# Where one queue issues attention stores and expert-weight loads, in an attention + MoE + dense-max kernel

## The chip, the cores and the metric

One core of one Trainium2 chip. The metric is device time in microseconds (us) of the whole kernel: 698.57 us, median of 3 runs (698.44 to 699.79).

## The reference, cut to what matters

Three stages, chained. Attention: 4 batches, 8 heads, 576 rows, head size 64, a causal window of 128 with a linear bias per head. Its output is a [2304, 512] matrix. A mixture of experts routes each row to one of 8 experts; then a dense layer takes the maximum of three products.

```python
# attention, for each batch and head
scores = where(0 <= rel < 128, q @ k.T / 8 - slope[h] * abs(rel), -1e9)
x = softmax(scores) @ v                       # -> [2304, 512]
# experts
e_idx = argmax(x @ w_gate + bias[modality]); gate = softmax(...)[e_idx]
out[e_idx == e] = gate * (relu(x[e_idx == e] @ w1[e]) @ w2[e])     # 512 -> 1024 -> 512
# dense layer
h = max(max(x @ g1, x @ g2), x @ g3); y = h @ w_out                # 512 -> 768 -> 512
```

Products run in float16 as high and low parts, in three passes (`PASSES`), so every float32 weight is first turned into two float16 tiles.

## The kernel before, in words

The order of work on every engine is written out by hand; each engine and each queue runs its own list in that order, and semaphores hold an instruction until its inputs and its buffer are ready. Nearly all loads and stores are issued by SyncE (SP), one after another: an issue that waits for a buffer holds all that are behind it.

**Attention.** `Attention.run` makes 41 steps. A step takes one group of four heads of one 128-row tile and does a part of several groups at once. `norm` (L426), early in a step, writes the finished rows into the tile `x` on VectorE (L436) and then issues the store of `x` to the scratch matrix `xs` (L443, L448) on SP; 16 full stores and 4 pairs of small ones in all. At the end of a step the list `todo` runs: loads of raw k, q and v (L274, `load`, seven to five steps ahead of use, three buffers for each), their transposes (`turn`, L283 on TensorE), and the splitting of v.

**Experts.** Rows are sorted by expert and cut into four batches (u = 0 to 3) of one or two units each: 496 | 480, 224 | 496 | 496, 192 columns. A unit needs 8 pieces of weights of 512 KB (four of `w1`, four of `w2`), so 48 pieces, here called P0 to P47. A piece is loaded into one of three buffers `st` (L945), converted to its high part on ScalarE (L954) and to its low part on VectorE (L963, which frees the buffer). `Weights.get(n)` (L969) runs ahead of the products that use piece n (twice for a `w1` piece, once for a `w2` piece): it converts the low part of piece n+1 and the high part of piece n+2, and then issues the load up to piece n+4. A product (L991 first layer, L1010 second) is split by ScalarE (`hf` L981, then L982) and GpSimd (L983). The second layer leaves `yT` in four blocks (dm = 0 to 3), which the dense layer reads.

**Interleaving.** The units of batches 0 and 1 run between attention steps: `layer1` (L1411) makes a step about every three and a half us of expert work. Attention ends within the 480 unit; its memory is then given to the dense layer, whose 24 weight loads (here W0 to W23; L1065, L1071, `Weights2`) go through four buffers `st2` and are put together from their bits on VectorE (L1105, L1110, L1116), scaled and split on ScalarE (L1133, L1134) and GpSimd (L1135). `tick` and `finish`, called in `layer1` after each block of products, do this bit by bit; a load W is issued behind the L1116 that frees its buffer. The dense layer for batches 0 and 1 follows (products L1150, maxima L1159, output L1195), then the expert layers of batches 2 and 3, where four more buffers serve the pieces (`more`), then the second dense layer.

In SP's list, around the end of attention, the loads stand so: P18, W0 to W3, P19, W4, W5, P20 to P24, W6, W7, P25, P26, P27, W8 and so on. P25 is issued in `get(21)`, which serves dm = 1 of the 224 unit; the high parts of P24 and P25 are converted in `get(22)` and `get(23)`, on ScalarE ahead of the splits of dm = 2 and dm = 3.

Of the kernel before, what the change touches and what calls it, by code (L numbers as in the profile page):

```python
# [15 lines left out]
B, H, S, D = 4, 8, 576, 64  # L16
# [31 lines left out]
def windowed_attention_moe_kernel(  # L48
# [16 lines left out]
    nc = tc.nc  # L65
# [11 lines left out]
    xs = [dram.tile([HALF, DM], F32, name=f"xs{h}") for h in range(2)]  # L77
# [33 lines left out]
    class Bias:  # L111


        def __init__(self, pool, pf, bias, nq, widths):
            self.bias, self.nq = bias, nq
            tot = sum(widths)
            self.rf = pf
            if nq < 128:
                self.rf = pool.tile([128, 1], F32, name=f"c_rf{nq}")
                nc.vector.tensor_copy(self.rf[0:nq], pf[0:nq])  # L120
                nc.vector.tensor_scalar(self.rf[nq:], pf[nq:], float(-nq), None, ALU.add)
            self.ci = pool.tile([128, tot], I32, name=f"c_ci{nq}")
            o = 0
            for w, base in zip(widths, (-WIN, 0)):
                nc.gpsimd.iota(
                    self.ci[:, o:o + w], base=base,
                    pattern=[[1, w]], channel_multiplier=0,
                )
                o += w
            self.rel = pool.tile([128, tot], F32, name=f"c_rel{nq}")  # L130
            self.t = pool.tile([128, tot], F32, name=f"c_t{nq}")
# [88 lines left out]
    def drain(gen):  # L220
        for _ in gen:
            pass
# [29 lines left out]
    class Attention:  # L252
# [5 lines left out]
        def __init__(self, pool):  # L258
            self.p = pool
            self.bias = pool.tile([128, H, 256], BF16, name="bias", bufs=1)  # L260
            self.biast = pool.tile([128, 4, 192], BF16, name="biast", bufs=1)
            self.raw, self.qT, self.kT, self.v = {}, {}, {}, {}
            self.xs, self.got = {}, set()
            self.mixed = False
            self.outs = []

        def rows(self, t):
            return 128 if t < 4 else 64
# [157 lines left out]
        def norm(self, b, t, g, ps):  # L426
            p = self.p
            if g == 0:
                self.xs[b, t] = p.tile([128, 2, 4, D], F32, name="x", tag="x", bufs=2)
            x = self.xs[b, t]  # L430
            rd = p.tile([128, 4, 1], F32, name="rd", tag="rd", bufs=2)
            nc.vector.tensor_scalar(rd, ps[:, :, D:D + 1], SV / SX * 1e-9, None, ALU.add)
            yield
            nc.vector.reciprocal(out=rd, in_=rd)
            yield
            nc.vector.tensor_tensor(  # L436
                out=x[:, g], in0=ps[:, :, 0:D], in1=rd.to_broadcast([128, 4, D]),
                op=ALU.mult,
            )
            dst, r = xs[b // 2], S * (b % 2)  # L440
            if t == 4:
                for u in range(2):
                    nc.sync.dma_start(  # L443
                        out=dst[r + 512:r + S, 256 * u:256 * u + 256],
                        in_=x[64 * u:64 * u + 64, 0].rearrange("p b c -> p (b c)"),
                    )
            elif g == 1:
                nc.sync.dma_start(  # L448
                    out=dst[r + 128 * t:r + 128 * t + 128, :],
                    in_=x.rearrange("p a b c -> p (a b c)"),  # L450
                )

        def xt(self, t, x):
            kd = KD if t < 4 else KD // 2
# [30 lines left out]
        def run(self):  # L485
            grp = [(b, t, g) for b in range(B) for t in range(5) for g in range(2 if t < 4 else 1)]
            todo = {}

            def at(n, f, *a):
                todo.setdefault(max(n, 0), []).append((f, a))  # L490

            for n, (b, t, g) in enumerate(grp):
                if g:
                    continue
                if n >= 4:
                    for x, nm in enumerate("kqv"):
                        at(n - LEAD + x, self.load, nm, b, t)
                if n:
                    at(n - 4, self.turn, "k", b, t)
                    at(n - 3, self.turn, "q", b, t)  # L500
                at(n - 2, self.high_v, b, t)
                at(n - 2 + (n > 1), self.low_v, b, t)
            ss, es, ehl, xts, lgs, pvs = {}, {}, {}, {}, {}, []
            N = len(grp)
            for n in range(N + 5):
                norm = iter(())
                if n < N:
                    if n not in ss:
                        ss[n] = self.qk(*grp[n])
                    pvs.append(n)  # L510
                if n in lgs and (self.mixed or n >= N):
                    self.logits(*lgs.pop(n))
                    self.logits_out()
                due = [m for m in pvs if m <= n - 3]
                for m in due:
                    pvs.remove(m)
                    drain(norm)
                    self.low(ehl[m])
                    norm = self.norm(*grp[m], self.pv(*grp[m], ehl.pop(m)))
                if self.mixed and 0 <= n - 1 < N:  # L520
                    ehl[n - 1] = self.transpose(*grp[n - 1], es.pop(n - 1))
                if n < N:
                    es[n] = self.softmax(*grp[n], ss.pop(n), norm)
                if not self.mixed and n + 1 < N:
                    ss[n + 1] = self.qk(*grp[n + 1])
                for _ in norm:
                    fill()
                if n in lgs:
                    self.logits(*lgs.pop(n))
                if n - 2 in ehl:  # L530
                    self.low(ehl[n - 2])
                self.logits_out()
                if not self.mixed and 0 <= n - 1 < N:
                    ehl[n - 1] = self.transpose(*grp[n - 1], es.pop(n - 1))
                if 0 <= n - 1 < N:
                    self.high(ehl[n - 1])
                for m in due:
                    b, t, g = grp[m]
                    if g or t == 4:
                        xts.setdefault(n + (t < 4), []).append((b, t, self.xs.pop((b, t))))  # L540
                for b, t, x in xts.pop(n, ()):
                    if n + 1 in lgs:
                        self.logits(*lgs.pop(n + 1))
                    lgs[n + 1] = (b, t, self.xt(t, x))
                if self.mixed and n - 1 in ehl:
                    self.low(ehl[n - 1])
                for f, a in todo.pop(n, ()):
                    f(*a)
                yield n

        def start(self):
# [363 lines left out]
    class Weights:  # L915
# [51 lines left out]
                self.whole += 1  # L967

        def get(self, n):  # L969
            self.low(n + 2)  # L970
            self.high(n + 3)
            self.issue(n + (9 if self.more else 5))
            return self.wt[n]

    def slot(pool, wst, w0, xT, yT, d, cap):
# [163 lines left out]
    def moe2(pool, items, w, hmt, n2=C2, both=False, **kw):  # L1139
# [5 lines left out]
        def product(run, yT, c, m, i):  # L1145
            ps = psM.tile([128, 512], F32, name="m", tag="m")[:, 0:n2]
            n = 0
            for kk in range(KD):
                for wl, xl in PASSES:
                    nc.tensor.matmul(  # L1150
                        out=ps, lhsT=w.g[:, wl, i, m, kk, :],
                        rhs=yT[:, xl, kk, c:c + n2], start=(n == 0), stop=(n == 3 * KD - 1),
                    )
                    n += 1
            nx = pool.tile([128, C2], F32, name="hx", tag="hx", bufs=4)[:, 0:n2]
            if i == 0:
                nc.scalar.activation(out=nx, in_=ps, func=ACTF.Copy, scale=2.0 ** -6)
            else:
                nc.vector.scalar_tensor_tensor(  # L1159
                    out=nx, in0=ps, scalar=2.0 ** -6, in1=run, op0=ALU.mult, op1=ALU.max  # L1160
                )
            return nx
# [344 lines left out]
```

## Time and profile before

| | |
|---|---|
| median of 3 runs | 698.57 us (698.44 to 699.79) |
| the profiled execution | 693.81 us, its span 691.9 us |
| TensorE (PE) busy | 645.2 us, 93% of the span |
| VectorE (DVE) / ScalarE (ACT) / GpSimd (POOL) busy | 353.6 / 345.3 / 226.6 us |
| granted TensorE clock | 0.983 of full speed over the span |
| bytes moved | 69.95 MB, mean 101 GB/s |

Times in the rows are microseconds from the first instruction of the span. SPq is the queue of SyncE, on which the DMAs are issued. A timeline row has start, duration, engine, line, operation, output and input; in square brackets stands the idle time of the engine just before it and what ended it. The chain is the work that ended last, followed back from the last instruction.

### The profile page before, as it was taken

The page shows a single profiled execution, that of the slowest core. Times are in us where ns is not written, and L with a number is a line of the kernel's source. Part 1 is how long each engine was busy: PE and PEld are TensorE (multiplying, and loading weights), DVE is VectorE, ACT ScalarE, POOL GpSimd, SP SyncE. Part 2 cuts the span into 40 slices and gives each one's busy share as a digit, 9 for nine tenths or more (in the row PEclk, how much of TensorE's full clock was granted, in tenths as well). Part 3 has the DMA queues.
Part 4 walks back from the last instruction along what each step waited for, and adds up shares of the span by engine and source line. Part 5 has one row for each costly group of instructions (what it writes and reads, how often), then busy time and mean ns, then how long its engine had stood idle before and what let it go on. Part 6 is the DMA issues. An engine that isn't in the chain of part 4 may idle for free.

```text
span 691.9 us, 12893 instructions
## 1 busy us (share of the span) xinstructions
PE 645.2 (93%) x4787; PEld 400.0 (58%) x4787; DVE 353.6 (51%) x1083; ACT 345.3 (50%) x660; POOL 226.6 (33%) x232
## 2 busy tenths in 40 slices
PE   6899888989997999899889999999999999999993
PEld 5687755656664656755555564444447656656641
DVE  5977864666475738999981233152324455201100
ACT  5898877777584837654552211354647211111110
POOL 2111226323131315766672311482424111121121
PEclk9999999999998999999999999999999999999997
DMA  9655773545330238664733403344240000000011
GB/s 192 108 124 133 195 200 87 119 113 164 106 91 20 78 117 272 214 203 162 190 113 76 92 22 122 119 127 120 91 117 8 1 0 1 1 31 16 0 47 49
DMA packets 120800, 69.95 MB, mean 101 GB/s; under 512 B 68872, under 2 KB 115484, under 8 KB 120732
## 3 DMA queue, kind: packets, MB, share of 16 engines
q1 hardware_dynamic: 116992, 59.06, 32.3%
q0 software_dynamic: 3040, 9.96, 4.6%
q8 instruction: 40, 0.66, 0.4%
q14 instruction: 28, 0.23, 0.1%
q10 hardware_dynamic: 700, 0.04, 0.1%
HBM read 57.19 MB, written 9.44 MB: 96 GB/s over the span
## 4 chain that ended last, share of the span: by engine, by line
PE 73%; DVE 12%; ACT 6%; DMA 3%; issue 3%; POOL 0%; ACTq 0%; SPq 0%; POOLq 0%; DVEq 0%
PE m L1150 25%; PE m L991 13%; PE m L1010 12%; PE m L1195 10%; PE s L335 4%; DMA st<-in_moe_w_dram 2%; PE m L376 2%; PE m L468 2%; DVE b L1110 2%; PE m L283 2%; PE bank L406 2%; DVE e L348 2%; ACT e L357 2%; ACT eh L382 1%; DVE wt L963 1%
## 5 line engine op out<-in xcount | busy, mean ns | idle before, releaser
L1150 PEld LDWEIGHTS <-g 128*128 128x128 f16 x1296 | 127.2, 98 | 93.8 <-issue 11.3
L1150 PE MATMUL m<-yT,g 128*128 128x384 f16 x648 | 109.1, 329 | 7.3 <-DVE hx L1159 2.9
L1150 PE MATMUL m<-yh,g 128*128 128x384 f16 x648 | 105.7, 326 | 0.0
L963 DVE SCALAR_TENSOR_TENSOR wt<-st,wt 128x1024 f16<-128x1024 f32 x48 | 61.9, 1293 | 79.3 <-ACT wt L954 79.3
L1010 PE MATMUL m<-ht,wt 128*128 128x496 f16 (+3 forms) x576 | 100.3, 333 | 1.7 <-DVE el L387 1.2
L1159 DVE SCALAR_TENSOR_TENSOR hx<-m,hx 128x384 f32<-128x384 f32 x72 | 39.7, 555 | 116.7 <-PE m L1150 116.7
L991 PEld LDWEIGHTS <-wt 128*128 128x128 f16 x576 | 55.6, 99 | 55.4 <-issue 9.3
L1010 PEld LDWEIGHTS <-wt 128*128 128x128 f16 x576 | 54.6, 98 | 43.4 <-issue 2.8
L983 POOL TENSOR_TENSOR ht<-hf,ht 128x496 f16<-128x496 f32 (+3 forms) x48 | 49.5, 1036 | 89.3 <-ACT ht L982 85.7
L981 ACT ACTIVATE hf<-m 128x496 f32<-128x496 f32 (+3 forms) x72 | 35.8, 497 | 76.2 <-PE m L1010 47.5
L357 ACT ACTIVATE e<-e,nm 128x256 f32<-128x256 f32 (+2 forms) x144 | 59.2, 471 | 21.1 <-DVE nm L348 20.9
L991 PE MATMUL m<-xT,wt 128*128 128x496 f16 (+2 forms) x288 | 58.5, 347 | 7.3 <-DVE el L387 3.8
L348 DVE CUSTOM_DVE_ANT_0 e<-s,bias 128x256 f32<-128x256 f32 (+1 forms) x128 | 45.8, 382 | 19.9 <-PE s L335 11.7
L991 PE MATMUL m<-xh,wt 128*128 128x496 f16 (+1 forms) x288 | 51.1, 330 | 0.0
L954 ACT ACTIVATE wt<-st 128x1024 f16<-128x1024 f32 x48 | 50.0, 1045 | 2.0 <-DMA st<-in_moe_w_dram 1.7
L387 DVE TENSOR_TENSOR el<-m,eh 128x512 f16<-128x512 f32 x64 | 42.4, 683 | 7.1 <-ACT eh L382 7.1
L1181 POOL TENSOR_TENSOR xh<-hx,xh 128x384 f16<-128x384 f32 x18 | 16.4, 913 | 89.8 <-ACT xh L1180 89.8
L335 PE MATMUL s<-kT,qT 64*128 64x256 f32 (+2 forms) x320 | 42.2, 384 | 3.3 <-DVE nm L348 2.2
L1180 ACT ACTIVATE xh<-hx 128x384 f16<-128x384 f32 x18 | 9.4, 523 | 70.8 <-DVE hx L1159 66.9
L311 POOL TENSOR_TENSOR vl<-rawv,vh 128x512 f16<-128x512 f32 (+1 forms) x20 | 23.0, 1149 | 65.7 <-ACT vh L304 65.7
L1201 ACT ACTIVATE ob<-m,gate 128x512 f32<-128x512 f32 x18 | 12.4, 687 | 55.0 <-PE m L1195 49.6
L382 ACT ACTIVATE eh<-m 128x512 f16<-128x512 f32 x64 | 34.6, 584 | 4.3 <-PE m L376 4.1
(184 smaller groups left out, 976.3 us busy)
## 6 DMA issues: line engine op xcount, KB each, us to landing
st<-in_moe_w_dram SPq DMA_DIRECT2D x66, 512.0 KB, 4.0
rawk<-in_k_dram SPq DMA_DIRECT2D x16, 256.0 KB, 4.5
rawq<-in_q_dram SPq DMA_DIRECT2D x16, 256.0 KB, 5.1
rawv<-in_v_dram SPq DMA_DIRECT2D x16, 256.0 KB, 3.5
xs<-x SPq DMA_DIRECT2D x16, 256.0 KB, 2.2
st<-in_moe_w_out_dram SPq DMA_DIRECT2D x6, 512.0 KB, 3.9
rawk<-in_k_dram SPq DMA_DIRECT2D x4, 128.0 KB, 4.5
rawq<-in_q_dram SPq DMA_DIRECT2D x4, 128.0 KB, 3.8
```

Source lines behind the costliest of these rows:

```text
L335: nc.tensor.matmul(out=out[u][rows, x // 2, c0:c1], lhsT=self.qT[b, t][r, i, 0:n], rhs=self.kT[b][r, i, k0 + c0:k0 + c1], start=True, stop ...
L348: nc.vector.tensor_tensor_reduce(out=e[:, x, c0:c1], in0=s[x % 2][:, x // 2, c0:c1], in1=bias[:, x, c0:c1], scale=-0.125, scalar=3.0e38, o ...
L357: nc.scalar.activation(out=e[:, x, c0:c1], in_=e[:, x, c0:c1], func=ACTF.Exp, scale=-1.0, bias=nm[:, x:x + 1],)
L382: nc.scalar.activation(out=b, in_=a, func=ACTF.Copy)
L387: nc.vector.tensor_tensor(out=o, in0=a, in1=b, op=ALU.subtract)
L954: nc.scalar.activation(out=wt[:, 0], in_=st, func=ACTF.Copy, scale=SW)
L963: nc.vector.scalar_tensor_tensor(out=wt[:, 1], in0=st.rearrange("p (a b) -> p a b", a=a), scalar=SW, in1=wt[:, 0], op0=ALU.mult, op1=ALU.s ...
L983: nc.gpsimd.tensor_tensor(out=lo, in0=hf, in1=hi[1], op=ALU.subtract)
L991: nc.tensor.matmul(out=ps, lhsT=wt[:, wl, kk, o:o + 128], rhs=xT[:, xl, kk, bass.ds(d[0], cap)], start=(n == 0), stop=(n == 3 * KD - 1),)
L1010: nc.tensor.matmul(out=ps, lhsT=wt[:, wl, f, :], rhs=hs[f][:, xl], start=(n == 0), stop=(n == 3 * KF - 1),)
L1150: nc.tensor.matmul(out=ps, lhsT=w.g[:, wl, i, m, kk, :], rhs=yT[:, xl, kk, c:c + n2], start=(n == 0), stop=(n == 3 * KD - 1),)
L1195: nc.tensor.matmul(out=ps, lhsT=hm[:, xl, f, 128 * u:128 * u + 128], rhs=w.wo[:, wl, f, :], start=(n == 0), stop=(n == 3 * K2 - 1),)
```

## The change

The store of a finished attention tile is no longer issued within `norm`: `norm` puts it on a list, and a new function `store` issues all stores on the list at the end of the step, behind the loads of later tiles. `Weights.get` issues loads first instead of last, and one piece fewer: up to piece n+3 ahead of the conversions of `get(n)`, where it was up to piece n+4 behind them (with the four additional buffers up to n+7, where it was n+8).

```diff
-            self.outs = []
+            self.outs, self.stores = [], []
...
-            dst, r = xs[b // 2], S * (b % 2)
-            if t == 4:
-                for u in range(2):
+            self.stores.append((b, t, g, x))
+
+        def store(self):
+
+            while self.stores:
+                b, t, g, x = self.stores.pop(0)
+                dst, r = xs[b // 2], S * (b % 2)
+                if t == 4:
+                    for u in range(2):
+                        nc.sync.dma_start(
+                            out=dst[r + 512:r + S, 256 * u:256 * u + 256],
+                            in_=x[64 * u:64 * u + 64, 0].rearrange("p b c -> p (b c)"),
+                        )
+                elif g == 1:
                     nc.sync.dma_start(
...
                 for f, a in todo.pop(n, ()):
                     f(*a)
+                self.store()
                 yield n
...
         def get(self, n):
+            self.issue(n + (8 if self.more else 4))
             self.low(n + 2)
             self.high(n + 3)
-            self.issue(n + (9 if self.more else 5))
             return self.wt[n]
```

## Rows read from the trace of the kernel before

**Rows 1.** Busy time by stretch: length; PE, PEld, DVE, ACT, POOL; clock, DMA share, GB/s
```profile
258.00:296.00 38.00, 33.95 (x280) 24.38 (x279) 33.80 (x77) 24.34 (x45) 22.95 (x18) 1.00 0.71 225
296.00:360.00 64.00, 59.14 (x358) 34.52 (x356) 60.45 (x81) 32.76 (x61) 42.58 (x33) 0.98 0.60 179
360.00:678.00 318.00, 317.96 (x1834) 176.21 (x1833) 92.49 (x241) 100.24 (x173) 90.65 (x90) 1.00 0.19 55
```

**Rows 2.** Waits of PE, DVE, ACT, ended by loads or unexplained: total us, times, longest
```profile
PE m L283 <- DMA rawk<-in_k_dram: 4.2, 1, 4.2
...
DVE b L1105 <- DMA st<-in_moe_w_dram: 3.9, 1, 3.9
...
PE m L283 <- issue: 3.4, 2, 1.9
...
ACT wt L954 <- DMA st<-in_moe_w_dram: 1.7, 1, 1.7
```

**Rows 3.** Waits of the SP queue itself, the same columns
```profile
SPq L945 <- DVE wt L963: 175.4, 36, 21.3
...
SPq L448 <- DVE x L436: 99.6, 16, 17.4
```

**Rows 4.** Timeline around the longest store wait: SP queue, then ACT
```profile
204.56 0.37 SPq L945 DMA_DIRECT2D st<-in_moe_w_dram  x1
...
222.44 0.34 SPq L448 DMA_DIRECT2D xs<-x  x1
...
230.67 1.05 ACT L954 ACTIVATE wt<-st 128x1024 f16<-128x1024 f32 x1
```

**Rows 5.** Timeline around a transpose of raw k: SP, DVE, PE
```profile
126.71 0.66 SPq L274 DMA_DIRECT2D rawk<-in_k_dram  x1
...
150.48 0.69 DVE L387 TENSOR_TENSOR el<-m,eh 128x512 f16<-128x512 f32 x1 [0.51 <-ACT eh L382]
...
151.27 0.63 PE L283 MATMUL m<-ident,rawk 128*128 128x128 f32 x4 [1.90 <-issue]
```

**Rows 6.** The chain of waits from 284 to 302: start, us, what
```profile
285.53 6.22 DMA st<-in_moe_w_dram
...
294.98 6.07 PE m L1150 x26
```

**Rows 7.** Timeline of the SP queue behind the end of attention
```profile
258.08 2.04 SPq L1065 DMA_DIRECT2D st<-in_moe_w_dram  x4
...
264.89 0.38 SPq L945 DMA_DIRECT2D st<-in_moe_w_dram  x1
266.81 0.97 SPq L1065 DMA_DIRECT2D st<-in_moe_w_dram  x2
...
282.02 0.38 SPq L945 DMA_DIRECT2D st<-in_moe_w_dram  x1
283.80 0.98 SPq L1065 DMA_DIRECT2D st<-in_moe_w_dram  x2
...
285.53 0.38 SPq L945 DMA_DIRECT2D st<-in_moe_w_dram  x1
```

**Rows 8.** Timeline of ACT: conversions of P19, P24 and P25
```profile
271.62 1.04 ACT L954 ACTIVATE wt<-st 128x1024 f16<-128x1024 f32 x1
...
288.32 1.04 ACT L954 ACTIVATE wt<-st 128x1024 f16<-128x1024 f32 x1
...
291.77 1.06 ACT L954 ACTIVATE wt<-st 128x1024 f16<-128x1024 f32 x1 [1.74 <-DMA st<-in_moe_w_dram]
```

**Rows 9.** DMA traffic in two stretches, columns as in Rows 1
```profile
259.40:265.40 6.00, 6.00 (x32) 2.77 (x31) 3.11 (x5) 2.12 (x3) 1.04 (x1) 1.00 1.00 340
283.10:292.20 9.10, 8.16 (x77) 7.04 (x75) 9.03 (x22) 6.74 (x13) 7.62 (x5) 1.00 0.89 289
```

**Rows 10.** Timeline of DVE: low parts of P19 and P20; first dense maximum
```profile
276.06 2.77 DVE L963 SCALAR_TENSOR_TENSOR wt<-st,wt 128x1024 f16<-128x1024 f32 x2
...
301.15 0.56 DVE L1159 SCALAR_TENSOR_TENSOR hx<-m,hx 128x384 f32<-128x384 f32 x1 [0.49 <-PE m L1150]
```

More of the change, by code (lines that the diff above doesn't have):

```diff
@@ L439, in norm @@
             )
-            dst, r = xs[b // 2], S * (b % 2)
-            if t == 4:
-                for u in range(2):
+            self.stores.append((b, t, g, x))
[10 more added lines that the diff above has]
+                elif g == 1:
                     nc.sync.dma_start(
-                        out=dst[r + 512:r + S, 256 * u:256 * u + 256],
-                        in_=x[64 * u:64 * u + 64, 0].rearrange("p b c -> p (b c)"),
-                    )
[L447 to L451, printed above, removed]
+                        out=dst[r + 128 * t:r + 128 * t + 128, :],
+                        in_=x.rearrange("p a b c -> p (a b c)"),
+                    )
         def xt(self, t, x):
```

## The prediction, made before the changed kernel had run

> **What bounds the kernel now.** I read the table of busy time by stretch first, then the waits, then the chain, then the timelines of SP, ACT and DVE. From 360 us on TensorE is busy for 317.96 of 318 us [rows 1]: nothing there is won by issuing a load elsewhere, and any time lost or gained before 360 us arrives at the end in full. From 296 to 360 VectorE is busy for 60.45 of 64 us and TensorE for 59.14; in that stretch VectorE puts the dense weights together and TensorE waits for them. From 258 to 296 VectorE is again the fullest (33.80 of 38) after TensorE.
>
> The change touches only SP's list, so the question is who waits for SP. SP itself waits a lot, 175.4 us for buffers of expert weights and 99.6 us for finished attention rows [rows 3]; that looks like a prize. But the compute engines wait for a load from SP in three places only [rows 2]: 4.2 us for the first raw k at the start of the run (ahead of any store), 3.9 us for the first dense weights, and 1.7 us on ScalarE for one expert piece. The last one is on the chain: the DMA of P25, issued at 285.53, lands 6.22 us later, and the chain goes from it over ScalarE and GpSimd to the dense product that goes on at 294.98 [rows 6].
>
> **The change part by part.** It adds no instruction and takes none away; it reorders 24 stores, some 50 loads of k, q, v, and the loads from P4 on.
>
> *Stores behind the loads of their step.* Loads of raw tiles leave about a step earlier, the stores where VectorE has written the row, as before. Nothing waited for a raw tile after the start [rows 2], so the gain is nothing. Stores are read back by GpSimd's gathers much later, and [rows 2] holds no wait that a store ended: cost nothing. Ends: the third rival prices a gain; a loss would need a raw tile to be late, and none leaves later than it did.
>
> *Pieces one `get` later, while attention runs.* The buffer of a piece is free just as early as before, but in SP's list the piece now stands behind the stores of the step in between. ScalarE converts piece j in `get(j-2)`; it used to be issued in `get(j-4)` and is now in `get(j-3)`. The worst place is the store that left at 222.44: P13 left at 204.56, and will leave just behind that store, at about 222.9. With a landing as slow as the 6.22 us of [rows 6] it is there at 229.1; ScalarE converts it at 230.67 [rows 4]. The cover is 1.6 us. I take nothing; if the cover were gone (a landing half as long again, at 232.2), ScalarE and the products behind it would be late by 1.6 us.
>
> *Pieces behind the dense weights, 258 to 296.* Here SP's list holds the loads W. The new order is W0 to W3, P18, W4, W5, P19 to P23, W6, W7, P24, P25, P26: each piece that stood ahead of a batch of W now stands behind it. In the first half that costs ScalarE some waiting (second rival) that VectorE, busy with other work, hides in my reading. In the second half it meets the chain. P24 left at 282.02, W6 and W7 at 283.80, P25 at 285.53 [rows 7]. W6 waits for VectorE's L1116, so P24 will leave behind it at about 284.8; P25 still leaves at about 285.5, when its buffer is free.
>
> What P25 then costs, step by step. Between 283.1 and 292.2 the DMA engines moved 9.1 us x 289 GB/s = 2.63 MB [rows 9], which is five transfers of 512 KB (P24, W6, W7, P25, P26): 1.82 us each. P25, the fourth, had its data by 283.1 + 4 x 1.82 = 290.4 and landed at 291.75, 1.35 us later. In the new order the first of the four is W6. W0 was issued at 258.08 and data began to flow at 259.4 [rows 7, 9], so W6's data begin at 283.8 + 1.3 = 285.1; the DMA engines lie idle for the two us before. Four transfers at 1.82 us and 1.35 us to land: 293.7. At the best rate that rows show, 6.0 us for the four of W0 to W3 (340 GB/s, 1.5 us each), it is 292.45 with the same 1.35 us, and 291.1 with nothing for landing. I take 293.1, halfway between the two that count landing. P24 lands a transfer earlier, at 291.3 to 291.6, well after the 288.32 at which ScalarE converted it. From there ScalarE needs 291.77 - 1.74 - 288.32 = 1.71 us for that conversion and the split of dm = 2 [rows 8], so it is free for P25 at about 293.1 too. P25's conversion starts at 293.1 instead of 291.77: 1.3 us later. The ends are 0 (P25 there by 291.1 and P24 in time) and 2.0 us (293.7).
>
> Behind this conversion on ScalarE stands the split of dm = 3; for its two halves wait GpSimd's L983 and the dense products at 294.98. These get the 1.3 us. Does it pass on? The first maximum of the dense layer finds VectorE idle for 0.49 us, waiting for TensorE [rows 10], so VectorE has no slack to swallow it, and from there to 360 it is the full engine, in a fixed order. It passes.
>
> A rule of the Trainium skill speaks against this. The page "DMA: Bandwidth & Descriptors", section "Anatomy of one DMA", gives a transfer 2.0 us plus its bytes over 436 GB/s; in sum four transfers of 512 KB would take 4.8 us of data, P25 would land by about 291.2 and the delay would be near nothing. The rows show 1.5 to 1.82 us for each where the rule has 1.2, so I go by the rows; the first rival is the case in which the rate is better than these.
>
> *P27 and the later pieces.* P27 no longer leaves in this stretch but before the second expert layer, where SP has nothing else to do and TensorE is full [rows 1]: nothing.
>
> Sum: +1.3 us on the profiled execution, 693.81 to 695.1. The median of the runs is 698.57, 4.8 us above the profiled one; I add the same 1.3 us to it: 699.9 us.
>
> **The rivals.**
>
> First, *no change*: P24 and P25 land in time, because with P19 and P27 out of the way the DMA engines move faster than 1.5 us a transfer, or VectorE's stretch from 301 us on gives the time back. For it: the 0 end above, and 59.14 of 64 us on TensorE leave it 4.9 us of idle time that VectorE sets. Against it: the 0.49 us. Time 698.6.
>
> Second, *slower by more*: P19. It left at 264.89, ahead of W4 and W5 (266.81); it will leave behind them, at 267.9. With 1.3 us until data flow from 266.81, three transfers at 1.5 to 1.82 us and 1.35 us to land it is there between 274.0 and 274.9; ScalarE converted it at 271.62 and will wait 2.4 to 3.3 us. VectorE takes its low part at 276.06 [rows 10] and needs ScalarE's 1.04 us first, so the point from which it costs is a landing at 275.0. My estimate is just under it. If it is past by 1.5 us (a transfer more in front), VectorE, full since 262, carries that to the end beside the 2.0 us of P25: 3.5 us, 702.1.
>
> Third, *faster*: twice, 3.4 us together [rows 2], TensorE stands still ahead of a transpose of raw k with no releaser shown; the longer is the 1.90 us before 151.27 [rows 5]. If these are late loads, held behind a store, loads ahead of stores win both: 695.2. It decides at a load landing later than the start of the gap (149.4). Against it: the last raw k issued by then with time to be this one left at 126.71, 22 us before, and the gap ends 0.1 us after VectorE's L387 (150.48 + 0.69 = 151.17), which frees a PSUM buffer. That the change doesn't reach what SP waits for is part of the first rival.
>
> **How the numbers follow.** Chances: forecast 0.40 (its own range 698.8 to 700.6), no change 0.27, slower by more 0.15, faster 0.18. 0.2% of the time, 1.4 us, is about what a measurement of this kernel can tell from none. The forecast's 1.3 us lies at that bound, so it gives 0.20 to same and 0.20 to slower. No change gives 0.22, 0.03 faster and 0.02 slower. Sums: faster 0.21, same 0.42, slower 0.37. The range goes from 696.2 (short of the third rival's full gain) to 702.2 (the second rival's sum).
>
> **What would show it.** Right: ScalarE's waits for expert pieces grow from 1.7 us to several us, at P19, P24 and P25; the dense product that stood at 294.98 goes on at about 296.3, and the end of that stretch (360 us) moves as much. SP's waits for rows and buffers shrink with no effect before 258 us. Wrong: a shorter stretch before 258 us (third rival, or something in attention that waits for SP without the profile naming it), P24 converted at 288 as before, or a stretch from 296 to 360 that is shorter than 64 us by what was lost.

## The result, and the profile after

The changed kernel is slower: 703.83 us median (701.65 to 708.04, 8 runs) against 698.24 us (695.12 to 699.79, 8 runs) beside it, ratio 1.009, 95% interval 1.0063 to 1.0118. The forecast was 699.9 with a range up to 702.2: the direction of the cost was right, its size four times too small. Ratios here and below leave out executions more than 1.5% above the fastest of the same kernel; medians take all.

In the changed file the lines stand lower: L945, L954, L963, L983 are now L952, L961, L970, L990; L1105, L1110, L1116, L1150, L1159 are now L1112, L1117, L1123, L1157, L1166. In the kernels of the experiments they stand up to two lines lower than in the kernel that was edited.

The profiled execution took 703.39 us, its span 701.6. Busy time by stretch, columns as in [rows 1]:

```profile
258.00:296.00 38.00, 35.57 (x294) 25.41 (x293) 28.78 (x63) 23.34 (x43) 21.17 (x17) 1.00 0.75 239
296.00:360.00 64.00, 54.52 (x326) 31.53 (x324) 54.91 (x85) 29.46 (x55) 39.92 (x28) 0.92 0.52 163
360.00:678.00 318.00, 315.46 (x1831) 175.99 (x1830) 100.88 (x251) 104.68 (x182) 97.34 (x94) 1.00 0.20 58
```

From 296 to 360 us TensorE is busy for 4.6 us less than in [rows 1], and at a lower mean clock. The waits that answer to [rows 2, 3]:

```profile
PE m L1157 <- POOL yT L990: 7.0, 2, 5.1
...
ACT wt L961 <- DMA st<-in_moe_w_dram: 5.3, 3, 2.3
...
PE m L283 <- issue: 3.4, 2, 1.9
...
SPq L952 <- DVE wt L970: 122.0, 24, 20.3
SPq L454 <- DVE x L436: 113.8, 15, 19.6
```

SP waits 53 us less for weight buffers and 14 us more for rows, to no one's use. ScalarE's waits for pieces grew from 1.7 to 5.3 us, as forecast. The first line is the news: TensorE waits up to 5.1 us for GpSimd's half of a split (the subtraction that makes the low part of `yT`). The chain of waits, answering to [rows 6]:

```profile
290.31 4.99 DMA st<-in_moe_w_dram
...
295.44 0.84 issue
...
297.25 1.46 POOL yT L990
298.71 0.56 issue
299.26 6.26 POOL yT L990
...
305.57 6.05 PE m L1157 x26
```

P24 lands, ScalarE converts it, and then GpSimd's half of dm = 3, begun at 299.26, takes 6.26 us. (The 1.46 us of dm = 2 are the part of that half that lies on the chain.) The timelines of GpSimd, both halves in one row, and of VectorE there:

```profile
297.19 8.32 POOL L990 TENSOR_TENSOR yT<-hf,yT 128x224 f32 x2 [1.58 <-ACT yT L989]
305.48 1.15 POOL L1142 TENSOR_TENSOR g<-b,g 128x512 f16<-128x512 f32 x1
...
299.49 1.27 DVE L1117 SCALAR_TENSOR_TENSOR b<-st,b 128x512 int32<-128x512 int32 x2
300.69 1.27 DVE L1123 SCALAR_TENSOR_TENSOR b<-st,b 128x512 int32<-128x512 int32 x2
301.89 0.74 DVE L1112 TENSOR_SCALAR b<-st 128x512 int32<-128x512 int32 x2
302.56 1.27 DVE L1117 SCALAR_TENSOR_TENSOR b<-st,b 128x512 int32<-128x512 int32 x2
303.76 1.27 DVE L1123 SCALAR_TENSOR_TENSOR b<-st,b 128x512 int32<-128x512 int32 x2
```

VectorE works on the dense weights' bits without a pause from 299.49 to 305.03, and GpSimd's half, begun at 299.26, ends at 297.19 + 8.32 = 305.51. In the kernel before, the same half, work of GpSimd and VectorE around it, and TensorE's wait stood so:

```profile
293.65 1.28 POOL L983 TENSOR_TENSOR yT<-hf,yT 128x224 f32 x1 [1.41 <-ACT yT L982]
...
298.38 3.30 POOL L1135 TENSOR_TENSOR g<-b,g 128x512 f16<-128x512 f32 x1 [3.46 <-ACT g L1134]
...
293.05 1.21 DVE L963 SCALAR_TENSOR_TENSOR wt<-st,wt 128x1024 f16<-128x1024 f32 x1
294.18 0.27 DVE L723 TENSOR_TENSOR r_rhs<-r_ot,parts 128x120 f16<-128x120 f16 x1
...
295.11 1.27 DVE L1110 SCALAR_TENSOR_TENSOR b<-st,b 128x512 int32<-128x512 int32 x2
...
294.98 6.07 PE L1150 MATMUL m<-yT,g 128*128 128x384 f16 x26 [1.10 <-POOL yT L983]
```

There the half ends at 294.93, 0.18 us before VectorE begins. Even its 1.28 us are not those of a half left alone: VectorE's L963 and L723, each with two inputs, run until 294.45, and the half ends 0.48 us behind them. And L1135 on GpSimd, begun at 298.38 beside bit operations, takes 3.30 us; in the kernel after, at 305.48, with VectorE idle, it takes 1.15. So the trace before already showed what the late half would meet.

The span of this profile is longer by 9.7 us, the medians by 5.6. About 4 us of the difference come from one earlier place: the first three conversions of pieces stand at 99.97 instead of 96.09, behind two pauses of VectorE. The first, near 86 us, is shown; ahead of the same instruction the kernel before waits 0.48 us. The second is 2.15 us near 93 us, where the kernel before waits 0.84:

```profile
88.99 0.16 DVE L432 TENSOR_SCALAR rd<-bank 128x4 f32<-128x4 f32 x1 [3.14 <-PE m L376]
```

These explanations stood before the experiments. *Theory A*: the late loss comes from P24 behind W6 and W7 and from GpSimd held off by VectorE; the early 4 us come from the stores' move. *Rivals*: B, the early 4 us come and go with the execution; C, the loss is that of P18 and P19, for which ScalarE also waited (1.34 and 1.73 us); later D, lateness passes on at its own size.

To compare profiles without the early part, one figure serves below, the **stage**: from the start of P17's conversion on ScalarE to the dense layer's first maximum on VectorE (L1159, in the changed file L1166). It is 301.15 - 261.69 = 39.46 us before [rows 10] and 311.73 - 265.52 = 46.21 us after.

### The profile page after: what moved, and what is told of

The parts are those of the page before. It is cut to its first block, busy times and chain, and to the rows that moved or that the text cites. A ratio compares the mean times of both kernels' runs of the same rounds, so it can differ in the third digit from the quotient of the medians.

```text
span 701.6 us, 12887 instructions
## 1 busy us (share of the span) xinstructions
PE 646.5 (92%) x4787; PEld 400.8 (57%) x4787; DVE 351.6 (50%) x1083; ACT 346.0 (49%) x660; POOL 229.9 (33%) x232
## 4 chain that ended last, share of the span: by engine, by line
PE 73%; DVE 10%; ACT 7%; DMA 3%; issue 3%; POOL 1%; SPq 0%; ACTq 0%; POOLq 0%; DVEq 0%
PE m L1157 26%; PE m L998 12%; PE m L1017 12%; PE m L1202 9%; PE s L335 3%; PE m L376 2%; DMA st<-in_moe_w_dram 2%; PE m L474 2%; PE bank L406 2%; PE m L283 2%; DVE e L348 2%; ACT e L357 2%; DVE b L1117 1%; DVE el L387 1%; ACT eh L382 1%
## 5 line engine op out<-in xcount | busy, mean ns | idle before, releaser
L1157 PEld LDWEIGHTS <-g 128*128 128x128 f16 x1296 | 127.3, 98 | 98.8 <-issue 16.4
L1157 PE MATMUL m<-yT,g 128*128 128x384 f16 x648 | 109.4, 330 | 12.0 <-POOL yT L990 7.0
L1157 PE MATMUL m<-yh,g 128*128 128x384 f16 x648 | 105.7, 326 | 0.0
L970 DVE SCALAR_TENSOR_TENSOR wt<-st,wt 128x1024 f16<-128x1024 f32 x48 | 61.6, 1285 | 80.6 <-ACT wt L961 80.6
L1166 DVE SCALAR_TENSOR_TENSOR hx<-m,hx 128x384 f32<-128x384 f32 x72 | 39.7, 555 | 123.6 <-PE m L1157 123.6
L990 POOL TENSOR_TENSOR ht<-hf,ht 128x496 f16<-128x496 f32 (+3 forms) x48 | 50.6, 1061 | 89.8 <-ACT ht L989 87.7
L961 ACT ACTIVATE wt<-st 128x1024 f16<-128x1024 f32 x48 | 50.0, 1046 | 5.4 <-DMA st<-in_moe_w_dram 5.3
L376 PE MATMUL m<-ident,e 128*128 128x128 f32 (+1 forms) x256 | 35.8, 279 | 1.5 <-issue 0.9
```

The costliest lines, as they stand in the source:

```text
L376: nc.tensor.transpose(ps[:n, x, :], e[:, x, a:z], ident)
L961: nc.scalar.activation(out=wt[:, 0], in_=st, func=ACTF.Copy, scale=SW)
L970: nc.vector.scalar_tensor_tensor(out=wt[:, 1], in0=st.rearrange("p (a b) -> p a b", a=a), scalar=SW, in1=wt[:, 0], op0=ALU.mult, op1=ALU.s ...
L990: nc.gpsimd.tensor_tensor(out=lo, in0=hf, in1=hi[1], op=ALU.subtract)
L1157: nc.tensor.matmul(out=ps, lhsT=w.g[:, wl, i, m, kk, :], rhs=yT[:, xl, kk, c:c + n2], start=(n == 0), stop=(n == 3 * KD - 1),)
```

## The experiments

| kernel | ratio to before (95%) | stage, us |
|---|---|---|
| before, second profile | | 39.37 |
| after, second profile | | 46.62 |
| stores' order alone | 1.0009 (0.9982 to 1.0035) | 39.44 |
| new `get` alone | 1.0110 (1.0083 to 1.0136) | 46.18 |
| after, P24 on in the old order | 1.0002 (0.9971 to 1.0033) | 39.88 |
| after, P17 to P21 in the old order | 1.0066 (1.0037 to 1.0094) | 45.51 |
| after, VectorE waits for the half | 1.0041 (1.0021 to 1.0062) | 40.79 |
| before, P25 converted twice | 1.0037 (1.0002 to 1.0071) | 39.44 |
| before, P25 converted three times | 1.0100 (1.0068 to 1.0133) | 46.10 |
| before, P24 and P25 converted later | 0.9969 (0.9935 to 1.0003) | 37.56 |
| after, P24 and P25 converted later | 0.9964 (0.9935 to 0.9994) | 38.86 |

**Stores' order alone.** After's `norm` and `store`, with the old `get`:

```diff
         def get(self, n):
-            self.issue(n + (8 if self.more else 4))
             self.low(n + 2)
             self.high(n + 3)
+            self.issue(n + (9 if self.more else 5))
```

> The kernel before with the stores of attention rows moved behind the loads of their step, and nothing else of the change. Theory A (the change has two costs: about 4 us at 86 to 91 us of the span, where the stores' move lets loads and raw tiles be issued in one bunch, and about 5 to 6 us at 295 to 306 us, through GpSimd's halves of the last unit): only the first is left, time 3 to 4.5 us above before (about 702), the first conversion of an expert weight near 100 us of the span instead of 96.1, GpSimd's two halves at about 1.3 us each. Theory B (the early 4 us is a stall that comes and goes from run to run, whatever the kernel): 0 +- 1 us against before (about 698). Theory C (all of the loss comes from late conversions of pieces P18 and P19): 0.

693.49 against 693.47 us: nothing. The first conversions stand at 95.59. Theory A's early part fell.

**The new `get` alone.** The kernel before with only the change in `get`.

> The kernel after with the stores put back into their old place: only the new order within get (loads one piece further behind, issued at its start) is left. Theory A: the late loss alone, GpSimd's two halves of the last split together about 8 us instead of 2.6, the dense product's second half 5 to 6 us later than before against the start of the mixed phase; time about 5 us above before (about 703). Theory B: the late loss is the whole of the difference of the medians, 5 to 6 us above before. Theory C: the same size, but its gaps stand at P18 and P19 and the split itself is as short as before.

701.83 against 693.47 us: the whole loss, and its stage is that of after. GpSimd's two halves, VectorE's last bit operations, and TensorE:

```profile
293.04 1.32 POOL L983 TENSOR_TENSOR yT<-hf,yT 128x224 f32 x1 [2.37 <-ACT yT L982]
294.65 5.92 POOL L983 TENSOR_TENSOR yT<-hf,yT 128x224 f32 x1 [0.29 <-ACT yT L982]
...
298.81 1.27 DVE L1116 SCALAR_TENSOR_TENSOR b<-st,b 128x512 int32<-128x512 int32 x2
...
300.62 6.14 PE L1150 MATMUL m<-yT,g 128*128 128x384 f16 x26 [5.09 <-POOL yT L983]
```

The first half keeps its 1.3 us; only the last, begun beside the bit operations, takes 5.92.

**Second profiles of both kernels, unchanged.**

> The kernel before unchanged, for a second profile. If the stretch from 77 to 96 us of the span is the same from run to run (Theory A), the first three conversions of expert weights stand again at 96 us, VectorE waits no more than 0.5 us before the first reciprocal after the expert loads, and the span is 692 +- 1. If the early stall comes and goes (Theory B), it can stand at 99 to 100 with a span near 696.

> The kernel after unchanged, for a second profile. If the 4 us lost at 86 to 91 us in the first profile of after came with that execution alone (Theory B), VectorE waits here no more than 0.5 us before its reciprocal near 86.4, the first three conversions stand at 95 to 96.5 us, and the span is 695 to 698 with the loss of the last unit alone. If after has it each time (Theory A's early part), the conversions stand at 99 to 100 and the span is near 701.

Before: span 691.7, conversions at 96.02, as Theory A and B both allow. After: span 695.7, and no early pause; VectorE at 85.38 waited 0.49 us, the conversions stand at 94.99. The late loss is there again, first in the chain of waits, then VectorE's last bit operation from its timeline:

```profile
291.18 1.46 POOL yT L990
...
293.02 6.27 POOL yT L990
...
299.33 6.43 PE m L1157 x26
```

```profile
297.52 1.27 DVE L1123 SCALAR_TENSOR_TENSOR b<-st,b 128x512 int32<-128x512 int32 x2
```

So the early pauses came with that one execution. Steps of 3 to 4 us stand elsewhere too: with P25 converted three times, nothing of which touches that stretch, the fourth conversion came 17.1 us behind the first three instead of 15.7, and the fifth another 10.3 instead of 8.1. The profile of the next experiment shows the same step (17.0 and 10.3). What causes them is not settled.

**VectorE waits for the half.** After, with one small copy ahead of the dense product:

```diff
+        turnstile = m2.tile([128, 8], F16, name="turnstile", bufs=1)
+        nc.vector.tensor_copy(turnstile, yT[0][:, 1, KD - 1, WX[0]:WX[0] + 8])
         layer2(0, ...
```

> The kernel after, and VectorE reads eight columns of GpSimd's last half before it begins the dense weights' bit operations, so that it does not work beside that half. It adds one small copy on VectorE. Theory A (GpSimd is held up by VectorE's bit operations): the last two halves take about 1.3 us each again instead of 8.3 us together, the second half of the dense product starts 4 to 5 us earlier than after, and the time falls by 3 to 5 us against after (about 699). Theory C (the pieces' late landing costs it all, and the halves' length is only where it shows): no change against after within 1 us (about 704), the halves remain late, and VectorE loses the time that it waits.

697.45 us: of the loss of 0.9 to 1.1% (after, and the new `get` alone) 0.4% is left. Nothing in the loads' order changed; P24 still lands late.

```profile
296.94 3.19 POOL L990 TENSOR_TENSOR yT<-hf,yT 128x224 f32 x2 [1.06 <-ACT yT L989]
...
300.17 0.17 DVE L1467 COPY turnstile<-yT 128x8 f16<-128x8 f16 x1 [0.36 <-POOL yT L990]
300.25 1.29 DVE L1117 SCALAR_TENSOR_TENSOR b<-st,b 128x512 int32<-128x512 int32 x2
```

Both halves take 3.19 us together, and VectorE waited 0.36 us to save them 5. The stage is 40.79, 1.33 us above before: what lateness costs if GpSimd keeps its pace. That is 0.2% of the time; the rest of the 0.4% is not in the stage as profiled, and its cause is open.

**Which late pieces.** After, with one piece more issued at the end of four or five `get`s, as before (the first added pair of lines in one kernel, the second in the other):

```diff
             self.high(n + 3)
+            if 20 <= n < 24:
+                self.issue(n + 5)
...
+            if 12 <= n < 17:
+                self.issue(n + 5)
```

> The kernel after, but get(20) to get(23) also issue one piece more at their end, as before: P24 and the pieces behind it go out in the old order, ahead of W6 and W7; P17 to P23 stay late. Theory A (the loss comes from P24, issued behind W6 and W7, whose conversion stands ahead of the last split): the wait ahead of that conversion falls from 2.3 to about 1.7 us, GpSimd's last half is done ahead of VectorE's bit operations and takes 1.3 us, and the time is within 1 us of before. Theory C (P18 and P19, which waited 1.3 and 1.7 us): still 5 to 7 us above before.

> The kernel after, but get(12) to get(16) also issue one piece more at their end, as before: P17 to P21 go out in the old order, P24 stays behind W6 and W7. Theory A: the waits ahead of P18 and P19 go (1.3 and 1.7 us), yet the last half still takes 5 to 6 us and the time stays 5 to 7 us above before. Theory C: within 1 us of before.

With P24 and what is behind it in the old order the loss is gone (694.13 us) though ScalarE waited 2.03 us for P19; the half ends at 293.33, just ahead of the bit operations at 293.50. With P17 to P21 in the old order it stays (699.17). ACT, GpSimd and TensorE of the first, then GpSimd, VectorE's last bit operation and TensorE of the second:

```profile
272.21 1.06 ACT L961 ACTIVATE wt<-st 128x1024 f16<-128x1024 f32 x1 [2.03 <-DMA st<-in_moe_w_dram]
...
291.43 1.90 POOL L992 TENSOR_TENSOR yT<-hf,yT 128x224 f32 x1 [0.80 <-ACT yT L991]
...
293.38 5.82 PE L1159 MATMUL m<-yT,g 128*128 128x384 f16 x26 [1.72 <-POOL yT L992]
```

```profile
296.73 5.88 POOL L992 TENSOR_TENSOR yT<-hf,yT 128x224 f32 x1 [0.33 <-ACT yT L991]
...
300.87 1.27 DVE L1125 SCALAR_TENSOR_TENSOR b<-st,b 128x512 int32<-128x512 int32 x2
...
302.67 6.75 PE L1159 MATMUL m<-yT,g 128*128 128x384 f16 x26 [5.56 <-POOL yT L992]
```

Theory C fell.

**An edge, with no DMA moved.** Before, and ScalarE converts P25 two or three times, so that only the last split is late (the lines are those of three times):

```diff
                 nc.scalar.activation(out=wt[:, 0], in_=st, func=ACTF.Copy, scale=SW)
+                for _ in range(2 if self.done == 25 else 0):
+                    nc.scalar.activation(out=wt[:, 0], in_=st, func=ACTF.Copy, scale=SW)
```

> The kernel before, with no DMA moved: ScalarE converts P25 twice, so that the last split of the 224-token unit comes one conversion, about 1.05 us, later (GpSimd's last half begins near 294.7 instead of 293.65, VectorE's bit operations near 295.1 as before). Theory A (GpSimd's half is held off as soon as VectorE's bit operations run beside it, so a delay of 1 us goes over an edge): the half takes 5 to 6 us, the second part of the dense product begins near 300 instead of 295, and the time is 4 to 5.5 us above before. Theory D (the half is late in after because its pieces were late by that much; a delay passes on at its own size): the half takes 1.3 us, and the time is 0 to 1.2 us above before.

> As the run that converts P25 twice (whose executions fell into two groups, 691 to 693 and 696 to 703 us, with the profiled one in the lower), but P25 is converted three times: the last split of the unit comes about 2.1 us later than before, so that it lies beside VectorE's bit operations in every execution. Theory A (an edge): GpSimd's last half takes 5 to 6 us, the profiled execution shows TensorE's wait of about 5 us for it, the time from P17's conversion to VectorE's first running maximum (39.5 us before) is 45 to 46.5 us, and the median is 5 to 7.5 us above before, with no execution near 693. Theory D (the delay passes on at its own size): the half takes 0.6 to 1.3 us and the time is 1 to 2.2 us above before.

Twice: the 12 executions fell apart, four between 690.9 and 693.4 us and eight between 696 and 703 (median 699.21). The profiled one is of the first group; that the eight went over the edge is not shown, since none of them was profiled, and 4 of the 17 executions of before beside them also took 695.7 to 697.3. Three times: all six between 696.7 and 703.5, median 700.18 against 693.08. GpSimd's last half, VectorE and TensorE, twice and three times:

```profile
293.57 0.63 POOL L985 TENSOR_TENSOR yT<-hf,yT 128x224 f32 x1 [2.15 <-ACT yT L984]
...
293.89 1.46 DVE L1112 SCALAR_TENSOR_TENSOR b<-st,b 128x512 int32<-128x512 int32 x2
...
294.25 6.04 PE L1152 MATMUL m<-yT,g 128*128 128x384 f16 x26 [0.46 <-POOL yT L985]
```

```profile
301.06 3.53 POOL L985 TENSOR_TENSOR yT<-hf,yT 128x224 f32 x1 [4.95 <-ACT yT L984]
...
302.84 1.27 DVE L1118 SCALAR_TENSOR_TENSOR b<-st,b 128x512 int32<-128x512 int32 x2
...
304.64 7.06 PE L1152 MATMUL m<-yT,g 128*128 128x384 f16 x26 [3.21 <-POOL yT L985]
```

In the first the half began 0.32 us ahead of the bit operations and was done at once, and VectorE's first pair took 1.46 us instead of 1.27. In the second ScalarE had 2.1 us more to do, and P25 itself was there 1.2 us later, so that the half began 3.4 us later than before, counted from P17's conversion. It ended 5.6 us later, the 26 products behind it took 1.0 us more, and the stage grew by 6.6. Theory D fell, and Theory A's "5 to 6 us" for the half did too: it took 3.53. What holds is its end: 0.48 us after VectorE's last bit operation (304.59 and 304.11), as in after (305.51 and 305.03), its second profile (299.28 and 298.79), the new `get` alone (300.57 and 300.08) and P17 to P21 in the old order (302.61 and 302.14). The half comes through when VectorE stops, however late it began.

**P24 and P25 converted later, in both kernels.** P24 and P25 belong to the next unit; nothing in the 224 unit needs them. Into each kernel (into before also an upper bound of 27 on the issue, since P27 needs a buffer that is then freed later):

```diff
+            most = 24 if n < 24 else self.n
-            self.low(n + 2)
-            self.high(n + 3)
+            self.low(min(n + 2, most))
+            self.high(min(n + 3, most))
```

> The kernel before, but ScalarE converts P24 and P25 (and VectorE the low half of P24) not inside the 224-token unit but later in the dense product, where TensorE has work; the issue of P27 goes with them. Theory A (a conversion that waits for its piece ahead of a split is what decides when GpSimd's last half ends, and so when the dense product goes on): the 1.7 us wait ahead of the last split is gone, GpSimd's last half ends about 2 us earlier than 294.9, the dense product goes on near 293, and the time falls by 1.5 to 2.5 us against before. Theory C (only P18 and P19 count): no change within 0.7 us.

> The kernel after with the same edit: P24 and P25 are issued as late as after does, but converted later, in the dense product. Theory A: the whole loss is gone although P24 still lands late, since nothing ahead of the split waits for it; GpSimd's halves take 1.3 us each, and the time is 1 to 2.5 us below before. Theory C: 5 to 7 us above before, as after. Between them, if P18 and P19 cost 1 to 2 us that the tail does not win back: within 1 us of before.

692.31 and 692.79 us against 693.49. By its interval the second is faster than before by 0.06 to 0.65%, with every load issued as late as in after and a wait of 2.39 us at P19; the first has about the same gain, its interval just reaching 1. By the medians the first gains 1.2 us and the second 0.7, where 1.5 to 2.5 and 1 to 2.5 were expected. Of the 35 executions of before 14 took over 695 us, of the second version none of 12 (of the first 3). GpSimd's two halves and TensorE in after with the edit:

```profile
291.87 1.89 POOL L991 TENSOR_TENSOR yT<-hf,yT 128x224 f32 x2
...
293.19 5.00 PE L1158 MATMUL m<-yT,g 128*128 128x384 f16 x29 [0.51 <-POOL yT L991]
```

The halves come ahead of the bit operations (294.81 here). TensorE keeps its clock: 29 products in 5.00 us, where before 26 took 6.07 [rows 6]. Granted clock (third column from the end) in one us of before and two of before with the edit:

```profile
296.00:297.00 1.00, 1.00 (x5) 0.44 (x3) 1.00 (x3) 0.00 (x0) 0.00 (x0) 0.50 1.05 374
```

```profile
294.00:296.00 2.00, 2.00 (x14) 1.22 (x13) 2.00 (x5) 1.06 (x2) 0.00 (x0) 1.00 0.01 3
```

That is 1.2 GHz behind TensorE's waits of 0.5, 0.8 and 1.1 us for the splits, and 2.4 GHz behind one wait of 0.5 us.

## Why the prediction was wrong

- **Stores behind loads: nothing.** Right, shown: 1.0009 (0.9982 to 1.0035) alone.
- **Pieces one `get` later during attention: nothing.** Right. No conversion up to P17 waits for its piece in either profile of after. Later ones wait at P18, P19 and P24, in the second profile at P19, P22 and P24; the stage of before comes back when P24 on is restored, with all other pieces late.
- **P24 and P25.** Right to 0.3 us, in part by luck. P24's conversion was to come 3.0 to 3.3 us later and P25's 1.3; counted from P17's conversion they came 3.2 and 1.35 later (295.31 and 296.95 against [rows 8]), 3.4 and 1.55 in the second profile. But P24 left 24.79 us behind P17's conversion (290.31), where the working has 23.1 (284.8), and landed 4.99 us after its issue, where it has 6.5 to 6.8: two errors that nearly cancel. P25 was then late because ScalarE was; its conversion did not wait for its load.
- **"These get the 1.3 us."** This step failed. The lateness was passed through GpSimd's half of dm = 3 as if that half kept its 1.28 us, which already held a wait behind VectorE's L963 and L723. It had 0.18 us to spare before VectorE's bit operations; moved among them it ended where they end, and the stage grew by 6.75 us (7.25 between the second profiles). The term belongs at 6.7, not 1.3. Some of it comes back behind 306 us: between the second profiles the first maximum is 5.0 us later (305.87 and 300.87) and the span 4.0 us longer. Which engine was late next was asked for TensorE, ScalarE and VectorE, never for GpSimd beside VectorE.
- **The first rival, no change.** The order of the loads did cost, so no. From the issue of W6 (288.41) to the landing of P24, the third transfer, passed 6.9 us (7.1 in the second profile); the rows' best rate gives 1.3 + 3 x 1.5 + 1.35 = 7.15. (The Trainium skill's page "DMA: Bandwidth & Descriptors", section "Anatomy of one DMA", gives its figures for transfers that GpSimd issues, and these are SP's. By them, as an estimate, it would have been 5.6 us, which was too fast here.)
- **The second rival, P19.** Its wait was estimated at 2.4 to 3.3 us and just under the point from which it costs; measured 1.73 (after P18's 1.34) and 2.41, and no cost of it is measured (1.0002, 0.9971 to 1.0033, with P19 late).
- **The third rival, faster.** Refuted: TensorE's two unexplained pauses at raw k are the same 3.4 us, and the stores' order alone gives nothing.

## What to carry to other kernels

When work on GpSimd is moved in time, look at what VectorE does at the new time, not only at what waits for it: a duration read beside one neighbour is no price beside another. Where an operation ends a fraction of a microsecond before a long run of another engine, treat its lateness as an edge and price the far side. And before putting a prefetched conversion ahead of work on the chain, ask whether anything needs it there: taking it away gained more than either order of the loads.

## What the runs showed of the hardware

GpSimd's last subtraction of 128x224 took 0.63 to 1.90 us where it was done ahead of VectorE's bit operations and 3.5 to 6.3 us where it met them; in five profiles it ended 0.47 to 0.49 us behind the last of an unbroken run of them, as in the kernel before it ended 0.48 us behind L723. One that began 0.32 us ahead got through and lengthened VectorE's first pair by 0.19 us; one that began 0.23 us ahead (299.26 and 299.49) did not.

The Trainium skill has a rule for this, "SBUF — State Buffer", section "Who interferes with whom": a VectorE instruction with two inputs in SBUF contends with a GpSimd instruction that reads SBUF, and the one that comes first keeps the other out for its whole length. The traces agree as to who is kept out (L1117 and L1123 read `st` and `b`, both in SBUF), and the lengthened first pair shows VectorE kept out in its turn. As to how long, they show more than one instruction: GpSimd stayed out for all that was left of the run, up to five pairs of instructions one behind the other. That the shared port is the cause was not separated from other causes; that VectorE's run is what holds GpSimd follows from the copy that put it behind the half.
